# Idle matmuls on a tile that VectorE zeroes, and the last chain of block products in two PSUM banks

## The chip, the cores and the metric

The kernel runs on one core of a Trainium2 chip. The metric is device time in microseconds (us) of one execution; the median of three timed runs is compared. TensorE (PE, with its weight loads shown as PEld), VectorE (DVE), ScalarE (ACT), GpSimd (POOL) and the DMA queue of SyncE (SP) run at the same time and meet at semaphores.

## What is computed

Three stages in float32: causal attention blended with a memory term over 16 heads of 576 positions, a gated pair of dense layers, and a mixture of four experts with ReLU, weighted by normalised domain probabilities.

```
scores = q @ k.T / sqrt(D), causal;  a = softmax(scores);  local = a @ v
attn   = g * (phi(q) @ M_prev) / (phi(q) @ z_prev) + (1 - g) * local
x      = attn as [1152, 512]
x      = ((x @ w1) * (x @ w2)) @ w3 @ w_out
out    = sum over e of p[:, e] * (relu(x @ ew1[e]) @ ew2[e])     # 4 experts, 1024 wide
```

## The kernel before

**Order.** PE, ACT, DVE and POOL follow orders that are written out by hand: the list `FIRST` for the attention and the dense layers, the strings `START`, `CYCLE` and `END` for the experts. In `FIRST`, DMA issues on SP stand in the list too. Each engine executes its instructions in that order and waits where an operand or a buffer is not ready.

**The head.** The zeroing of buffers and the identity matrix `identF` are made by POOL: a memset of `identF`, a larger memset of `mask`, a select that leaves the diagonal. PE opens with 13 transposes of `identF` into a PSUM tile `warm` (lines 206 to 208); nobody reads `warm`. Then come the score products of the first pair of heads, `sc` (line 273), on the operands `qd` and `kd` that SP has loaded: eight float32 products for the first 512 positions, their halves on 64 of the 128 rows each, and two more over the last 64 positions (line 262). A float32 product that is not a transpose stands in the trace as two weight loads and two matmul records. DVE masks each block of scores, takes its minimum (`peaks`, line 289), ACT exponentiates it (line 294), PE transposes the result (`pt`, line 326), ACT copies it out (line 330). SP's load of the query tile two pairs on waits until the first pair's score products have released its buffer; the loads of weights behind it on SP wait with it.

**The experts.** Each expert's two layers are done in halves of its width with both layers cut into 2x2 blocks; a product of 2x2 blocks is made of seven block products. The first 640 tokens are plain in the second layer: five tiles `o` of 128 tokens and 512 columns (`plain_2`, line 1065), with an eviction each that adds to `acc`. The other 512 tokens use seven block products in `block_2` (line 1113). A product named P1 to P7 (F1 to F7 in the last round) is a list of twelve matmuls: two steps `y` (halves of the expert's width), three passes `x` of a float32 product split in high and low parts, and two halves `half` of 128 tokens. Its result stands in an accumulator `o_ps[d]`: d is 0, 1 or 2, each one PSUM bank with the two halves side by side, 256 columns each. The chain d = 0 runs 1, 6, 7, 4: it accumulates through all four, and its bank is added to `acc` after each of them by two evictions, one for each half (`evict`, line 1052, on DVE), scaled by `pr`.

**The banks.** `ps3` has the tags o0 to o4 and R. The plain tiles take o3, o4, o0, o1, o2 for i = 0 to 4; the last round of `block_2` has `banks=(3, 4, 0)`.

**The end.** The string `END` ends with F4: its twelve matmuls, with the halves taken in turn, then the evictions F4x and F4y. In the last round each eviction that completes a block of `acc` is followed by a store, issued by SP (`store`, line 1060). The eviction of the last plain tile (i = 4) is split there: ACT scales it into `part` (line 1086), POOL adds it.

Of the kernel before, what the change touches and what calls it, by code (L numbers as in the profile page):

```python
# [69 lines left out]
def kernel(  # L70
# [16 lines left out]
    nc = tc.nc  # L87
# [80 lines left out]
    A1 = attn.enter_context(tc.tile_pool(name="A1", bufs=1, side="right"))  # L168
    A2 = attn.enter_context(tc.tile_pool(name="A2", bufs=2, side="right"))
    identF = A1.tile([P, P], F32, name="identF")  # L170
    mask = A1.tile([P, S + P], F32, name="mask")
# [34 lines left out]
    warm = turn(psM, [P, 512], F32, "M", 2, "warm")  # L206
    for _ in range(13):
        nc.tensor.transpose(warm[:, 0:P], identF, identF)

# [855 lines left out]
    def plain_2(n):  # L1065

        e, _, j = steps[2 * n]
        q, res = e * NS + j, []
        for i in range(TILES):
            ps = {}  # L1070

            def mm(i, y, x, a, b, first, last, ps=ps):
                def f():
                    if first:
                        ps[0] = ps3.tile([P, 512], F32, tag=f"o{(i + 3) % TILES}", name=f"o{n}_{i}")
                    nc.tensor.matmul(  # L1076
                        ps[0], lhsT=h_of[2 * n + y][x][:, a, i * P : (i + 1) * P], rhs=w2s[q + y][x][:, b, :],
                        start=first, stop=last,
                    )
# [33 lines left out]
    def block_2(n, banks=(0, 1, 2), pre="P"):  # L1113
# [4 lines left out]
        def prod(d, a, b, first):  # L1118
            def mm(y, x, half):
                ia, ib = PASSES[x]  # L1120
                k, h = LOC[b]
                def f():
                    if first and y == x == half == 0:
                        o_ps[d] = ps3.tile([P, 2, HD], F32, tag=f"o{banks[d]}", name=f"ob{n}_{d}")
                    nc.tensor.matmul(  # L1125
                        o_ps[d][:, half], lhsT=h_of[2 * n + y][a][:, ia, half * P : (half + 1) * P],
                        rhs=w2s[q + y][k][:, ib, h * HD : (h + 1) * HD],
                        start=first and y == 0 and x == 0, stop=(y == 1 and x == 2), skip_group_check=True,
                    )
                return f  # L1130
            return [mm(y, x, half) for y in range(2) for x in range(3) for half in range(2)]

        def out_of(d, p, h, first, done=None):
            def half_of(half):
                def f():
                    t = TILES + 2 * p + half
                    evict(acc[t][:, h * HD : (h + 1) * HD], o_ps[d][:, half], t, e, start and first)
                    if last and done:
# [21 lines left out]
    def step(s, seg):  # L1160
# [135 lines left out]
        l41 l42 l43 l44 l45 l4E F50 F51 F52 F60 F61 F62 F53 F54 F55 F5E F63 F64 F65 F6E F20 F21 F22 F23 F24 F25 F2E F70  # L1296
        F71 F72 F73 F74 F75 F7E F30 F31 F32 F33 F34 F35 F3E F40 F41 F42 F43 F44 F45 F4x F4y
    """
# [118 lines left out]
```

## Time and profile before

| | |
|---|---|
| timed runs, median of 3 | 670.37 us (668.66, 670.37, 670.57) |
| the profiled execution, its own time | 668.36 us |
| its span, first to last instruction | 666.6 us |
| PE busy | 658.6 us, 99% of the span |
| DVE, ACT, POOL busy | 500.8, 368.6, 293.2 us |
| chain that ended last, by engine | PE 89%, DVE 6%, ACT 3%, DMA 1%, issue 1% |

The profiled execution's own time is 1.76 us more than its span. The chain that ended last is followed back from the last instruction: at each step the profile goes to the work that released it. An engine's busy time counts from the start of a record to its end; matmul records overlap, so that the distance between starts, and not the length of a record, is the time that each of them takes of the engine.

### The profile page before, as it was taken

To read this page: it belongs to the slowest core of one execution; us is meant where nothing else is said; L and a number is where in the kernel's file an instruction comes from. 1 tells how busy PE (TensorE), PEld (TensorE's weight loads), DVE (VectorE), ACT (ScalarE), POOL (GpSimd) and SP (SyncE) were. 2 spreads that over 40 slices of the span, in tenths; PEclk is the share of its full clock that TensorE was granted. 3 is DMA by queue.
4 is the path that set the end of the run, shared out by engine and by line. 5 is a ranking of instruction groups with operands and counts; after the bars stand their busy time and mean duration, and the time that the engine had idled before them with its cause. 6 is when DMAs were issued, how large, how long until landed. Compare 5 with 4: busy or idle time off the path is not lost.

```text
span 666.6 us, 13313 instructions
## 1 busy us (share of the span) xinstructions
PE 658.6 (99%) x5165; PEld 610.9 (92%) x5165; DVE 500.8 (75%) x1021; ACT 368.6 (55%) x780; POOL 293.2 (44%) x307
## 2 busy tenths in 40 slices
PE   8999999999999999999999999999999999999997
PEld 6778899989999999998899998998998999999997
DVE  5989997898849498577777666776767677676766
ACT  6998987757626364365544454355444444444441
POOL 2037646654443121725353545445454534555410
PEclk9999999999999999999999999999999999999999
DMA  8676266534511040120220211211212102111003
GB/s 280 204 250 191 103 202 180 158 116 159 191 65 64 32 157 3 32 95 1 64 64 2 95 32 31 64 32 33 64 33 64 57 8 94 33 33 32 1 32 111
DMA packets 34767, 57.78 MB, mean 87 GB/s; under 512 B 13456, under 2 KB 14480, under 8 KB 34704
## 3 DMA queue, kind: packets, MB, share of 16 engines
q1 hardware_dynamic: 34704, 56.93, 26.8%
q8 instruction: 40, 0.66, 0.4%
q14 instruction: 23, 0.19, 0.1%
HBM read 50.37 MB, written 6.55 MB: 85 GB/s over the span
## 4 chain that ended last, share of the span: by engine, by line
PE 89%; DVE 6%; ACT 3%; issue 1%; DMA 1%; POOL 0%; SPq 0%; DVEq 0%; POOLq 0%; ACTq 0%
PE o L1076 16%; PE Z L1184 15%; PE ob L1125 12%; PE c L608 8%; PE Q L1184 7%; PE ab L558 7%; PE wacc L494 5%; PE Zb L901 4%; PE R L1184 4%; PE pt L326 2%; PE Qb L901 2%; PE sc L273 2%; PE a L349 1%; DVE P L289 1%; PE Rb L901 1%
## 5 line engine op out<-in xcount | busy, mean ns | idle before, releaser
L1076 PE MATMUL o<-w,h 128*128 128x512 f32 x480 | 122.6, 393 | 0.0
L124 POOL TENSOR_TENSOR w<-r,w 128x512 fp32r<-128x512 f32 x48 | 68.1, 1425 | 97.8 <-ACT w L756 97.8
L1076 PEld LDWEIGHTS o<-w,h 128*128 128x128 f32 x480 | 85.3, 188 | 14.6 <-DVE w L127 0.2
L1125 PE MATMUL ob<-w,hS 128*128 128x256 f32 x384 | 55.2, 282 | 0.0
L558 PE MATMUL ab<-xT,ws 128*128 128x288 f32 x384 | 53.5, 297 | 0.0
L608 PE MATMUL c<-hT,W 128*128 128x288 f32 (+2 forms) x384 | 53.2, 295 | 0.0
L558 PEld LDWEIGHTS ab<-xT,ws 128*128 128x128 f32 x384 | 51.4, 188 | 0.7 <-issue 0.2
L608 PEld LDWEIGHTS c<-hT,W 128*128 128x128 f32 x384 | 51.8, 188 | 0.1
L1125 PEld LDWEIGHTS ob<-w,hS 128*128 128x128 f32 x384 | 51.0, 190 | 0.1
L1184 PE MATMUL Z<-X0T,w 128*128 128x320 f32 x288 | 50.4, 310 | 0.3
L494 PE MATMUL wacc<-wo,w3s 128*128 128x512 f32 x192 | 49.8, 403 | 0.0
L1047 ACT ACTIVATE h<-tt 128x320 fp32r<-128x320 f32 x48 | 22.6, 472 | 47.4 <-DVE tt L1220 21.7
L1056 DVE SCALAR_TENSOR_TENSOR acc<-ob,pr,acc 128x256 f32<-128x256 f32 x104 | 44.1, 476 | 5.9 <-PE ob L1125 5.9
L127 DVE TENSOR_TENSOR w<-r,w 128x512 fp32r<-128x512 f32 x64 | 47.1, 747 | 0.0
L1050 DVE SCALAR_TENSOR_TENSOR h<-tt,h 128x320 fp32r<-128x320 f32 x48 | 27.2, 566 | 25.8 <-ACT h L1047 25.8
L1184 PEld LDWEIGHTS Z<-X1T,w 128*128 128x128 f32 x288 | 40.4, 188 | 4.8 <-DVE X1T L127 0.8
L1125 PE MATMUL ob<-w,hA 128*128 128x256 f32 x288 | 44.3, 282 | 0.0
L1184 PEld LDWEIGHTS Z<-X0T,w 128*128 128x128 f32 x288 | 42.9, 188 | 1.1 <-ACT tt L1205 0.7
L1184 PE MATMUL Z<-X1T,w 128*128 128x256 f32 x288 | 42.1, 282 | 0.4 <-DVE X1T L127 0.4
L1205 ACT COPY tt<-Z 128x320 f32<-128x320 f32 (+1 forms) x32 | 12.8, 400 | 53.4 <-PE Z L1184 53.4
L494 PEld LDWEIGHTS wacc<-wo,w3s 128*128 128x128 f32 x192 | 34.3, 188 | 7.9 <-POOL w3s L124 0.8
L1207 DVE TENSOR_TENSOR tt<-tt,Q 128x320 f32<-128x320 f32 (+1 forms) x32 | 14.5, 453 | 35.2 <-ACT tt L1205 35.1
(198 smaller groups left out, 1585.6 us busy)
## 6 DMA issues: line engine op xcount, KB each, us to landing
w3r<-in_moe_w_tiles_dram SPq DMA_DIRECT2D x16, 512.0 KB, 4.0
wr<-in_moe_w_tiles_dram SPq DMA_DIRECT2D x16, 512.0 KB, 4.0
r<-in_moe_w_tiles_dram SPq DMA_DIRECT2D x32, 256.0 KB, 2.9
r<-in_moe_w_dram SPq DMA_DIRECT2D x32, 256.0 KB, 2.9
wor<-in_moe_w_out_dram SPq DMA_DIRECT2D x8, 512.0 KB, 5.1
wf<-tf SPq DMA_DIRECT2D x16, 256.0 KB, 4.2
wr<-wf SPq DMA_DIRECT2D x16, 256.0 KB, 2.9
qd<-in_q_cols_dram SPq DMA_DIRECT2D x8, 352.0 KB, 4.4
```

Of the source, the lines that this page charges most:

```text
L124: nc.gpsimd.tensor_sub(dst, src, r32(hi))
L127: nc.vector.tensor_sub(dst, src, r32(hi))
L494: nc.tensor.matmul(wacc[u], lhsT=w3s[u][:, a, c, :], rhs=wo[4 * g + c][:, bb, :], start=(c == 0 and x == 0), stop=(c == 3 and x == 2),)
L558: nc.tensor.matmul(ps[:, 0:HS], lhsT=self.ws[u][:, wi, kk, :], rhs=xT[b, kk][:, xi, a * HS : (a + 1) * HS], start=(n == 0), stop=(n == 3 * ...
L608: nc.tensor.matmul(st["ps"], lhsT=Wt[kk][:, wi, d * P : (d + 1) * P], rhs=hT[kk][:, xi, t0 : t0 + tw], start=(kk == 0 and x == 0), stop=(k ...
L901: nc.tensor.matmul(st[d], lhsT=b1_set[m][a][:, wi, kk, :], rhs=BX[b][:, xi, kk, :], start=first and kk == 0 and x == 0, stop=(kk == 1 and ...
L1047: nc.scalar.activation(h, src, AF.Relu)
L1050: nc.vector.scalar_tensor_tensor(out=h[:, 1], in0=src, scalar=0.0, in1=r32(h[:, 0]), op0=ALU.max, op1=ALU.subtract)
L1056: nc.vector.scalar_tensor_tensor(out=dst, in0=src, scalar=pr[:, t, e : e + 1], in1=dst, op0=ALU.mult, op1=ALU.add)
L1076: nc.tensor.matmul(ps[0], lhsT=h_of[2 * n + y][x][:, a, i * P : (i + 1) * P], rhs=w2s[q + y][x][:, b, :], start=first, stop=last,)
L1125: nc.tensor.matmul(o_ps[d][:, half], lhsT=h_of[2 * n + y][a][:, ia, half * P : (half + 1) * P], rhs=w2s[q + y][k][:, ib, h * HD : (h + 1) ...
L1184: nc.tensor.matmul(ps, lhsT=w1s[q][a][:, wi, kk, :], rhs=X[c, b][:, xi, kk, :], start=first and kk == 0 and x == 0, stop=(kk == 1 and x == ...
```

## The change

**The head.** A new tile `zw` of 128x128 float32 is zeroed by DVE, ahead of the other buffers. The 13 transposes of `identF` become 18 products of `zw` with its own first 64 columns.

**The last round's chain d = 0.** Its accumulator becomes two tiles of one bank each: half 0 in o3, half 1 in o2. To clear o2, the last plain tile of the last round (i = 4) takes o4 in place of o2 (`own`). Other rounds keep one bank for both halves.

**The last product.** F4's twelve matmuls are ordered by halves: six for half 0, then six for half 1. F4x, the eviction of half 0, is moved in front of F43 in `END`.

```diff
+    zw = A1.tile([P, P], F32, name="zw")
+    nc.vector.memset(zw, 0.0)
     identF = A1.tile([P, P], F32, name="identF")
...
     warm = turn(psM, [P, 512], F32, "M", 2, "warm")
-    for _ in range(13):
-        nc.tensor.transpose(warm[:, 0:P], identF, identF)
+    for _ in range(18):
+        nc.tensor.matmul(warm[:, 0:SB], lhsT=zw, rhs=zw[:, 0:SB], start=True, stop=True)
...
+        def own(i):
+            return 4 if i == 4 and e == E - 1 and j > 0 else (i + 3) % TILES
+
...
-                        ps[0] = ps3.tile([P, 512], F32, tag=f"o{(i + 3) % TILES}", name=f"o{n}_{i}")
+                        ps[0] = ps3.tile([P, 512], F32, tag=f"o{own(i)}", name=f"o{n}_{i}")
...
                     if first and y == x == half == 0:
-                        o_ps[d] = ps3.tile([P, 2, HD], F32, tag=f"o{banks[d]}", name=f"ob{n}_{d}")
+                        if last and d == 0:
+                            o_ps[d] = [ps3.tile([P, 512], F32, tag=f"o{z}", name=f"ob{n}_{d}_{z}")[:, 0:HD] for z in (3, 2)]
+                        else:
+                            ps = ps3.tile([P, 2, HD], F32, tag=f"o{banks[d]}", name=f"ob{n}_{d}")
+                            o_ps[d] = [ps[:, z] for z in range(2)]
                     nc.tensor.matmul(
-                        o_ps[d][:, half], lhsT=h_of[2 * n + y][a][:, ia, half * P : (half + 1) * P],
+                        o_ps[d][half], lhsT=h_of[2 * n + y][a][:, ia, half * P : (half + 1) * P],
...
+            if last and b == "T4":
+                return [mm(y, x, half) for half in range(2) for y in range(2) for x in range(3)]
             return [mm(y, x, half) for y in range(2) for x in range(3) for half in range(2)]
...
-                    evict(acc[t][:, h * HD : (h + 1) * HD], o_ps[d][:, half], t, e, start and first)
+                    evict(acc[t][:, h * HD : (h + 1) * HD], o_ps[d][half], t, e, start and first)
...
-        F71 F72 F73 F74 F75 F7E F30 F31 F32 F33 F34 F35 F3E F40 F41 F42 F43 F44 F45 F4x F4y
+        F71 F72 F73 F74 F75 F7E F30 F31 F32 F33 F34 F35 F3E F40 F41 F42 F4x F43 F44 F45 F4y
```

On PE at the start of the program, before (a row is one instruction or a run of like ones; behind a name stands its buffer number, in brackets what it waits for):

```order
L208 MATMUL warm_113<-identF_84 128x128 [waits Pool_49]
L208 MATMUL warm_113<-identF_84 128x128 x12
L273 MATMUL sc0_0_161<-kd0_147,qd0_145 128x128 [waits DMAHW1_49,DMAHW0_49]
L273 MATMUL sc0_0_161<-kd0_147,qd0_145 128x128
L273 MATMUL sc0_0_161<-kd0_147,qd0_145 128x256 x2
```

The same place after:

```order
L210 MATMUL warm_115<-zw_84 128x64 [waits DVE_49]
L210 MATMUL warm_115<-zw_84 128x64 x17
L275 MATMUL sc0_0_168<-kd0_154,qd0_152 128x128 [waits DMAHW1_49,DMAHW0_49]
L275 MATMUL sc0_0_168<-kd0_154,qd0_152 128x128
L275 MATMUL sc0_0_168<-kd0_154,qd0_152 128x256 x2
```

The idle matmuls now wait for DVE in place of POOL, there are five more of them, they have 64 columns, and they still stand ahead of the first score products.

On PE at the end of the program, products F3 (accumulator `ob15_2`) and F4 (`ob15_0`), before (`hA30`, `hS30` belong to step y = 0, `hA31`, `hS31` to y = 1):

```order
L1125 MATMUL ob15_2_8073<-w2_14_1_7710,hS30_7821 128x256 x6
L1125 MATMUL ob15_2_8073<-w2_15_1_7742,hS31_7928 128x256 [waits Activation_49]
L1125 MATMUL ob15_2_8073<-w2_15_1_7742,hS31_7928 128x256 x5
L1125 MATMUL ob15_0_7956<-w2_14_3_7862,hA30_7820 128x256 [waits DVE_49]
L1125 MATMUL ob15_0_7956<-w2_14_3_7862,hA30_7820 128x256 x5
L1125 MATMUL ob15_0_7956<-w2_15_3_7974,hA31_7927 128x256 x6
```

The same place after (`ob15_0_3` is half 0 in bank o3, `ob15_0_2` half 1 in o2):

```order
L1135 MATMUL ob15_2_8081<-w2_14_1_7717,hS30_7828 128x256 x6
L1135 MATMUL ob15_2_8081<-w2_15_1_7749,hS31_7935 128x256 x6
L1135 MATMUL ob15_0_3_7963<-w2_14_3_7869,hA30_7827 128x256 [waits DVE_49]
L1135 MATMUL ob15_0_3_7963<-w2_14_3_7869,hA30_7827 128x256 x2
L1135 MATMUL ob15_0_3_7963<-w2_15_3_7982,hA31_7934 128x256 x3
L1135 MATMUL ob15_0_2_7964<-w2_14_3_7869,hA30_7827 128x256 [waits DVE_49]
L1135 MATMUL ob15_0_2_7964<-w2_14_3_7869,hA30_7827 128x256 x2
L1135 MATMUL ob15_0_2_7964<-w2_15_3_7982,hA31_7934 128x256 x3
```

Twelve matmuls stay twelve; half 0 is complete six matmuls earlier, and each half waits for the eviction of its own bank alone.

On DVE at the end of the program, the last four evictions, before:

```order
L1056 SCALAR_TENSOR_TENSOR acc2_4506<-ob15_2_8073,pr_60,acc2_4506 128x256 [waits DVE_49,PE_49]
L1056 SCALAR_TENSOR_TENSOR acc2_4506<-ob15_2_8073,pr_60,acc2_4506 128x256 [waits DVE_49]
L1056 SCALAR_TENSOR_TENSOR acc3_4507<-ob15_0_7956,pr_60,acc3_4507 128x256 [waits PE_49]
L1056 SCALAR_TENSOR_TENSOR acc3_4507<-ob15_0_7956,pr_60,acc3_4507 128x256
L1412 UNCONDITIONAL_BRANCH
```

The same place after:

```order
L1058 SCALAR_TENSOR_TENSOR acc2_4513<-ob15_2_8081,pr_60,acc2_4513 128x256 [waits DVE_49,PE_49]
L1058 SCALAR_TENSOR_TENSOR acc2_4513<-ob15_2_8081,pr_60,acc2_4513 128x256 [waits DVE_49]
L1058 SCALAR_TENSOR_TENSOR acc3_4514<-ob15_0_3_7963,pr_60,acc3_4514 128x256 [waits PE_49]
L1058 SCALAR_TENSOR_TENSOR acc3_4514<-ob15_0_2_7964,pr_60,acc3_4514 128x256 [waits PE_49]
L1424 UNCONDITIONAL_BRANCH
```

The order of the evictions is the same; the last two wait for PE one by one, in place of both for the end of the whole product.

## Rows read from the trace of the kernel before

**Rows 1.** Stretches; busy us of PE, PEld, DVE, ACT, POOL; PEclk; DMA share; GB/s.

```profile
15.00:20.00 5.00, 4.78 (x36) 3.52 (x36) 4.88 (x19) 5.00 (x13) 0.72 (x1) 1.00 0.96 297
30.00:40.00 10.00, 9.78 (x102) 7.15 (x99) 9.82 (x32) 10.00 (x20) 1.89 (x2) 1.00 0.86 259
400.00:500.00 100.00, 100.00 (x673) 94.14 (x672) 70.14 (x135) 46.39 (x105) 51.24 (x56) 1.00 0.14 43
```

**Rows 2.** Chain that ended last, head: start us, us, what.

```profile
1.98 3.03 PE warm L208 x13
...
8.91 1.18 PE sc L262 x4
...
21.50 0.17 DVE gm L586
...
34.60 0.92 PE sc L273 x4
```

**Rows 3.** Timeline of the head: start us, us, engine, line, operation, operands, [idle before].

```profile
0.73 0.20 POOL masks.py:197 MEMSET identF<- 128x128 f32 x1 [0.29 <-POOLq L1377]
...
4.95 3.96 PE L273 MATMUL sc<-kd,qd 64*128 64x128 f32 x16
...
6.76 0.29 DVE L289 CUSTOM_DVE_ANT_0 P<-sc,mask 128x128 f32<-128x128 f32 x1 [0.96 <-PE sc L273]
...
7.09 2.55 ACT L294 ACTIVATE P<-P,mn 128x128 f32<-128x128 f32 x6 [2.58 <-DVE mn L289]
...
11.02 0.78 ACT L294 ACTIVATE P<-P,mn 128x576 f32<-128x576 f32 x1 [0.23 <-DVE mn L289]
```

**Rows 4.** PE records by form, 4.94 to 8.9 us, then 10.87 to 13.3 us.

```profile
L273 PE MATMUL sc<-kd,qd 64*128 64x384 f32 x4 | 1.5, 844 | 0.0
L273 PE MATMUL sc<-kd,qd 64*128 64x512 f32 x4 | 1.2, 698 | 0.0
...
L273 PE MATMUL sc<-kd,qd 64*128 64x512 f32 x4 | 1.1, 632 | 0.0
L273 PE MATMUL sc<-kd,qd 64*128 64x384 f32 x4 | 0.8, 482 | 0.0
```

**Rows 5.** Weight loads by form, 1.9 to 8.8, then 9 to 30 us; one chain piece.

```profile
L273 PEld LDWEIGHTS sc<-kd,qd 64*128 64x128 f32 x16 | 2.3, 326 | 1.1 <-issue 0.9
...
L349 PEld LDWEIGHTS a<-v,pT 128*64 128x64 f32 x135 | 4.1, 137 | 0.2 <-DVE tf_wo L156 0.2
...
L382 PEld LDWEIGHTS b<-mz,phi 128*128 128x128 f32 x8 | 1.0, 190 | 0.0
...
39.91 0.89 PE b L382 x8
```

**Rows 6.** Waits of SP in the first 60 us: total us, times, longest.

```profile
SPq L200 <- PE sc L262: 4.2, 1, 4.2
```

**Rows 7.** The end: timeline of ACT, PEld, DVE and SP.

```profile
656.11 0.68 ACT L1086 ACTIVATE part<-o,pr 128x512 f32<-128x512 f32 x1
...
656.81 1.51 PEld L1125 LDWEIGHTS ob<-w,hA 128*128 128x128 f32 x12
...
661.26 1.60 PE L1125 MATMUL ob<-w,hA 128*128 128x256 f32 x12
...
661.47 0.88 DVE L1056 SCALAR_TENSOR_TENSOR acc<-ob,pr,acc 128x256 f32<-128x256 f32 x2 [0.56 <-PE ob L1125]
662.90 0.88 DVE L1056 SCALAR_TENSOR_TENSOR acc<-ob,pr,acc 128x256 f32<-128x256 f32 x2 [0.56 <-PE ob L1125]
...
663.41 0.81 SPq L1063 DMA_DIRECT2D out_dram<-acc  x2
```

**Rows 8.** The end: chain that ended last; stores' time to landing.

```profile
654.22 8.66 PE ob L1125 x72
...
662.90 0.48 DVE acc L1056
...
DMA to landing us min/median/max: 1.7/2.0/2.4
```

## The prediction

> **What bounds the kernel now.** I read the stretches first. From 400 to 500 us PE is busy for 100.00 of 100 us; in the head it is not the bound: from 15 to 20 us ACT is busy for all 5.00 us and DVE for 4.88, from 30 to 40 us DVE for 9.82 of 10 [rows 1]. The chain that ended last says the same in order: idle matmuls from 1.98 us, the first score products, then ACT and DVE until the chain returns to PE at 34.60 us for good [rows 2]. So a shift of ACT's work in the first 12 us travels through ACT to 21.5 us, through DVE to 34.6, and then through PE to the end. In the head the reader is to see three places: DVE masks the first scores at 6.76 us, ACT has six exponentials from 7.09 to 9.64, and its next one on the chain, at 11.02, came after an idle time of only 0.23 us [rows 3].
>
> The second thing to see in the head is the speed of PE. The column PEclk reads 1.00, which is the level of 2.4 GHz, but the records speak against it: records of score products of 384 columns take 844 ns in the first set and 482 in the second; those of 512 columns, which come last in a set, take 698 and 632 [rows 4]. So PE runs at the level of 1.2 GHz through the idle transposes and the first products, and rises while the products of 512 columns run, near 8.2 us: some 6.2 us after the first idle transpose and 3.2 us after the first product (4.95 [rows 3]).
>
> **The change part by part: the head.** The memset of a 128x128 tile on POOL takes 0.20 us from 0.73 [rows 3]; DVE's masking of a 128x128 block takes 0.29, so zw is there at 0.93 to 1.02 and PE can begin at about 1.0 in place of 1.98 [rows 2]. The memset is first in DVE's queue; the next instruction there waits for an exponential of a loaded operand, so it costs DVE nothing. The first real transposes now carry the wait for POOL's identity, which PE had at 1.98 [rows 2]: nothing.
>
> What do 18 idle products take? Each float32 product is two records, as the sixteen records of the eight first score products show [rows 3], so there are 36 weight loads of 128 columns, each followed by a matmul of 64 columns. A load of 64 columns takes 137 ns and one of 128 columns 190 [rows 5]; the difference, 53 ns for 64 columns, makes 106 ns for 128 at the high level. The matmul beside it is shorter: eight records of 130 columns take 0.89 us, 111 ns each [rows 5], so 64 columns take some 54. The load is the longer of the two and sets the pace. At the low level loads of 128 columns take 326 against 190 ns [rows 5]; twice 106 is 213 ns, which I take. No row has loads as the bound at the low level: the pace lies between 106 ns (the matmuls, at half speed) and 320 (load and matmul one after the other). I take 213 because it is the one that follows from the rows of loads.
>
> When does the level rise? If the idle products count as the score products do, 3.2 us after 1.0: at 4.2. If it is the time since PE's first work of any kind, 6.2 us after: at 7.2. At 4.2 us 15 of 36 records are done and 21 remain at 107 ns: the idle products end at 6.45. At 7.2 us 29 are done: they end at 7.94. Score products can then start, 1.5 to 3.0 us later than before, but at the high level. From the first product to the first exponential it was 2.14 us (4.95 to 7.09 [rows 3]); the products of 128 and 256 columns, 384 of the 1280 columns that took 3.96 us, are 1.2 us of that, 1.4 since all of them ran at the low level, and half of this is saved: 2.14 - 0.7 = 1.4. From the first exponential to the end of ACT's work before 11.02 nothing changes (3.7 us). So the head moves by 6.45 + 1.4 - 7.09 - 0.23 = +0.5 us at the one end and 7.94 + 1.4 - 7.09 - 0.23 = +2.0 at the other; the 0.23 is ACT's idle time, which absorbs as much. I take +1.4, near the middle. SP's load of a later query tile waits 4.2 us for the first pair's products [rows 6], and the weights and keys behind it wait with it; with the first sixteen records in some 2.2 us at the high level and the last four in 1.18 [rows 2], these products end 9.8 to 11.3 against 10.09, which is less of a shift than ACT's, so SP adds nothing.
>
> The Trainium skill, in "TensorE: Matmul & The Clock Gate", Part 4 (PE-mode transpose), says that a transpose does not count as TensorE's activity for the clock as a product does. The trace agrees so far: PE was busy with transposes for 3 us and the level did not rise during them. By that rule alone the earlier end, +0.5 us, would hold.
>
> **The change part by part: the end.** Of the last twelve matmuls, from 661.26 and 0.12 us apart (72 in 8.66 us), half 0 is complete after six, at about 662.15. DVE is then busy with F3's evictions (661.47, two in 0.88 us) until 662.35, so F4x runs to 662.83 and is over before the last matmul ends at 662.88 [rows 7, 8]. F4y then starts at 662.90, where F4x started before; the two took 0.88 us in a row and one takes 0.48 [rows 7, 8], so the last eviction ends 0.40 us earlier. SP's last two stores were issued back to back from 663.41 in 0.81 us [rows 7], each behind its eviction; now F4x's goes out near 662.9 and the last one at 663.41, so that the last landing, 1.7 to 2.4 us behind its issue [rows 8], moves by 0.40 too. I take -0.4; the bounds are 0 (if the last store lands no earlier) and -0.5 (if the two stores also stop delaying each other).
>
> Three new waits go with it. F2, the chain d = 1, uses o4, which now holds the last plain tile, so it waits for ACT's `part`, which ends at 656.79; the loads of F2 began at 656.81 [rows 7]. With the time of a semaphore the delay is 0.05 us at most; behind it on PE stands everything to the end. F7 now waits for each half's eviction by itself, which can only be earlier. The last plain tile in o4 waits for the eviction of plain tile 1, long done. I take 0 for all, with +0.1 as their bound.
>
> **Sum.** 668.36 + 1.4 - 0.4 = 669.4 us, with 668.4 to 670.0 from the ends above; 670.3 if a wait at the end adds its bound and the last store nothing. The sum stands against the profiled execution (668.36), which is 2.0 us below the median of the timed runs (670.37). Two of these runs lie 2 us above the profiled one; a rise that comes later in some executions would do that, and would do it less after the change, but no row shows it. Against the median the forecast is -0.15%.
>
> **Rivals.** First, **the idle products are too thin to raise the level**: in each record PE streams for 107 of 213 ns, while in the score products and the transposes matmul follows on matmul. For it: nothing in the trace rises under such a stream. Against it: weights move all the time. Then all 36 records run at the low level, 36 x 0.213 = 7.7 us, to 8.7; the first exponential comes 2.14 us later, at 10.8; the head moves by 10.8 - 7.09 - 0.23 = +3.5 us, and by up to 2 us more if the rise falls behind the next four records (1.18 us at the high level [rows 2], as much again at half speed) and the transposes that follow. It gives 671.5 to 673.5, about 672.5: slower. It decides from the point at which the first score product starts after 8.5 us.
>
> Second, **the loads do not set the pace**: a record then takes 107 ns even at the low level, 36 take 3.85 us, and the idle products end at 4.85, before the score products began. With the level up at 4.2 the first exponential comes at 4.85 + 1.4 = 6.25, a gain of 0.84; with 7.2 the gain is 0.1. It gives 667.1 to 667.9, about 667.4: faster. Against it stands the difference of 53 ns between loads of 64 and 128 columns [rows 5]. The Trainium skill, in "TensorE: Matmul & The Clock Gate", LDWEIGHTS (loading the stationary operand), gives a load as its columns over 1.2 GHz, 107 ns for 128 at either level, and by that rule this rival would hold.
>
> Third, **the head does not reach the end**: DVE or PE has enough slack before 34.6 us to absorb the shift, and the change does only what its end part says, 668.36 - 0.4 = 668.0. Against it: ACT and DVE stand at 5.00 of 5 and 9.82 of 10 us [rows 1].
>
> **How the numbers follow.** Forecast 0.52, thin products 0.24, no load bound 0.14, head without effect 0.10. A measurement of this kernel can tell some 0.3% from no change, 2.0 us: faster is below 668.36, slower above 672.38. The forecast's own range, 668.4 to 670.3, lies within that, but for 0.04 below; the third rival sits just under the bound and gives half of its chance to faster, as does all of the second: faster 0.04 + 0.14 + 0.05 = 0.23, rounded to 0.22. Thin products give a little over half of their chance to slower, 0.13, and 0.01 comes from the other cases: 0.14. Same is the rest, 0.64. The predicted time is the forecast's, 669.4. The range reaches from 667.2 to 672.2: it leaves out about 0.04 of the second rival below and 0.13 of the first above.
>
> **What would show it.** In the profile of the changed kernel: PE's first record near 1.0 us; 36 idle records, and their end, at 6.4 to 7.9 (forecast), 8.7 (thin) or 4.9 (no load bound); the mean of the first products of 384 columns near 482 ns (forecast) or near 844 (thin); the first six exponentials from about 8.5 us in place of 7.09; ACT's next one at about 12.4 in place of 11.02; the chain's return to PE 1.4 us after 34.60. At the end: F4's two evictions 0.6 us apart, and the last store issued some 0.5 us after the last matmul, in place of 0.9. The forecast is wrong if the idle products end before 6 or after 8.5 us, or if the shift at 11 us is not found again at 35 us.

## The result and the profile after the change

The changed kernel takes 675.29 us (median of 6 runs, 674.24 to 676.26), the kernel before 669.93 beside it (6 runs): a ratio of 1.0083 (95% interval 1.0070 to 1.0095), slower by 5.4 us. The forecast was 669.4 and its range ended at 672.2, so it was wrong, and the time lies above the 671.5 to 673.5 of the first rival too. The profiled execution has 676.26 us and a span of 674.5.

PE in the head of the changed kernel (timeline; start us, us, engine, line, operation, operands, records, [idle before]):

```profile
1.05 7.94 PE L210 MATMUL warm<-zw 128*128 128x64 f32 x36 [1.05 <-DVE zw L171]
8.92 4.64 PE L275 MATMUL sc<-kd,qd 64*128 64x128 f32 x16
13.49 1.39 PE L264 MATMUL sc<-kd,qd 128*128 128x288 f32 x4
```

The tile of zeros is ready as early as forecast (first record at 1.05, not 1.98 [rows 2]). The 36 records then take until 8.99, and the first score product starts at 8.92 in place of 4.95 [rows 3]. The records by form from 8.9 to 13.5 us (busy us, mean ns) tell at which level PE ran:

```profile
L275 PE MATMUL sc<-kd,qd 64*128 64x512 f32 x4 | 1.9, 1057 | 0.0
L275 PE MATMUL sc<-kd,qd 64*128 64x384 f32 x4 | 1.5, 844 | 0.0
```

Before, those of 384 columns took 844 ns and those of 512 columns 698 in the first set, the last of them at the higher level already [rows 4]. Now both forms are at the level of 1.2 GHz. The trace's record of the granted clock gives the rise at 13.84 us, after all sixteen records; it was 8.10 before. So the new idle products not only took longer: the level did not rise during them, nor in the sixteen records after them.

ACT behind it (same columns), and SP's wait for the first pair's products (total us, times, longest):

```profile
11.07 2.55 ACT L296 ACTIVATE P<-P,mn 128x128 f32<-128x128 f32 x6 [6.81 <-DVE mn L291]
15.83 0.78 ACT L296 ACTIVATE P<-P,mn 128x576 f32<-128x576 f32 x1 [1.09 <-DVE mn L291]
```

```profile
SPq L202 <- PE sc L264: 9.3, 1, 9.3
```

The first exponential is 3.98 us later (11.07 against 7.09), the one of 576 columns 4.81 later (15.83 against 11.02 [rows 3]), SP waits 9.3 us instead of 4.2 [rows 6]. In the chain that ended last (start us, us, what) `gm` stood at 21.50 [rows 2] and is now 4.79 us later:

```profile
1.05 7.94 PE warm L210 x36
8.99 4.57 PE sc L275 x16
13.56 1.34 PE sc L264 x4
...
26.29 0.18 DVE gm L588
```

The chain runs through the idle products now, where it ran through the transposes: whatever they last too long, the kernel waits for.

Every later instruction of ACT can be set against the same one of before: the lag is 5.11 us at 33 us of the program before, 5.55 at 166, 6.12 at 189, 8.04 at 255, and 7.90 at the end. Most of the step to 8.04 is one wait near 249 us (same columns as SP's; 0.8 us before):

```profile
ACT w L758 <- DMA r<-in_moe_w_tiles_dram: 2.7, 1, 2.7
```

The end part did its work on DVE, as this timeline shows:

```profile
669.37 1.27 DVE L1058 SCALAR_TENSOR_TENSOR acc<-ob,pr,acc 128x256 f32<-128x256 f32 x3 [0.68 <-PE ob L1135]
670.80 0.48 DVE L1058 SCALAR_TENSOR_TENSOR acc<-ob,pr,acc 128x256 f32<-128x256 f32 x1 [0.17 <-PE ob L1135]
```

F4x now runs behind F3's evictions, in the group of three, and only one eviction is left after the last product. From ACT's `part` to the end of the last eviction it is 7.27 us (664.01 to 671.28), against 7.67 before (656.11 to 663.78 [rows 7]): 0.40 less. But the stores gave it back. From the end of the last eviction to the end of the span it is 3.2 us (674.5 - 671.28) and was 2.8 (666.6 - 663.78). This is SP's issue of the stores (duration ns min/median/max, first and last start us), and their time to landing:

```profile
L1065 SPq DMA_DIRECT2D out_dram<-acc x12: 333/390/1513, 658.6 to 671.8; - x12
...
DMA to landing us min/median/max: 1.8/2.2/4.1
```

Before, the longest landing was 2.4 [rows 8] and no issue behind 655 us took over 0.4 us. The landing of 4.1 us is not what the end waited for: that store was issued at 667.0 us and had landed by 671.1, and the last four took 1.8 to 2.0. What reached the end is the issue of 1.51 us: it held SP from 668.75 to 670.27, the four stores behind it went out 0.48 to 0.49 us apart, and the last one at 671.81, 0.53 us after the end of its eviction (0.06 before). What stood beside these stores is the last experiment's subject.

### The profile page after: what moved, and what is told of

It reads as the page before. It is cut to its first block, busy times and chain, and to the rows that moved or that the text cites. A ratio compares the mean times of both kernels' runs of the same rounds, so it can differ in the third digit from the quotient of the medians.

```text
span 674.5 us, 13362 instructions
## 1 busy us (share of the span) xinstructions
PE 664.9 (99%) x5188; PEld 616.3 (91%) x5188; DVE 503.7 (75%) x1022; ACT 368.7 (55%) x780; POOL 291.9 (43%) x307
## 4 chain that ended last, share of the span: by engine, by line
PE 87%; ACT 6%; DVE 3%; DMA 2%; issue 1%; SPq 0%; DVEq 0%; ACTq 0%
PE o L1082 16%; PE Z L1196 15%; PE ob L1135 12%; PE c L610 7%; PE Q L1196 7%; PE ab L560 6%; PE wacc L496 5%; PE R L1196 4%; PE Zb L903 3%; PE pt L328 2%; PE a L351 2%; PE sc L275 2%; PE Qb L903 1%; ACT P L296 1%; ACT pT L332 1%; PE warm L210 1%
## 5 line engine op out<-in xcount | busy, mean ns | idle before, releaser
L296 ACT ACTIVATE P<-P,mn 128x128 f32<-128x128 f32 (+4 forms) x72 | 37.5, 584 | 7.9 <-DVE mn L291 7.9
```

Of the source, the lines that this page charges most:

```text
L296: nc.scalar.activation(Pt[i, x], Pt[i, x], AF.Exp, bias=one, scale=-1.0)
```

## The experiments

The table gives for each the idle work in front (records of products are written weight columns x moving columns), from the profiled execution the start of the first score product, the rise of the level by the trace's clock record, the start of ACT's 576-column exponential, and ACT's lag against the kernel before at 33, 189 and 291 us (an instruction's start minus that of the same one before), and the ratio of the times with its interval.

| kernel | idle work | score | rise | 576 | lag 33/189/291 | ratio |
|---|---|---|---|---|---|---|
| before | 13 transposes | 4.95 | 8.10 | 11.02 | 0 | 1 |
| after | 36 of 128x64 | 8.92 | 13.84 | 15.83 | 5.1/6.1/8.0 | 1.0083 [1.0070, 1.0095] |
| e8, after again | the same | 8.92 | 14.10 | 15.96 | 5.0/7.5/7.3 | one run, 675.2 us |
| e2, without end part | the same | 8.92 | 11.85 | 14.88 | 4.4/6.8/8.2 | 1.0088 [1.0063, 1.0113] |
| e4 | 18 of 128x64 | 5.08 | 9.93 | 11.96 | 0.9/1.7/2.0 | 1.0005 [0.9988, 1.0021] |
| e12 | 80 of 128x64 | 18.30 | 21.12 | 24.22 | 13.2/14.4/15.3 | one run, 683.0 us |
| e3 | 18 of 128x128 | 5.18 | 7.05 | 10.86 | -0.2/1.6/2.1 | 0.9978 [0.9963, 0.9993] |
| e11, e3 again | the same | 5.19 | 5.58 | 10.33 | -0.2/0.6/0.4 | 0.9993 [0.9980, 1.0007] |
| e5 | 38 of 128x128 | 7.71 | 5.74 | 12.67 | 1.8/3.6/4.1 | 1.0046 [1.0030, 1.0063] |
| e6 | 36 of 64x64 | 5.08 | 5.05 | 10.03 | -0.4/1.2/2.1 | 1.0016 [1.0000, 1.0032] |
| e10, e6 again | the same | 5.08 | 6.50 | 10.73 | 0.0/1.1/1.5 | 1.0029 [1.0016, 1.0041] |
| e13 | 18 of 64x64 | 4.61 | 10.09 | 11.79 | 0.8/3.0/3.4 | 0.9997 [0.9982, 1.0011] |
| e14 | 26 of 64x64 | 4.71 | 4.03 | 9.67 | -1.4/0.1/1.3 | 1.0006 [0.9988, 1.0024] |
| e7 | none | 4.83 | 8.85 | 11.34 | 0.4/2.4/2.3 | 1.0015 [1.0001, 1.0028] |
| e1, end part alone | 13 transposes | 4.94 | 6.26 | 10.54 | -0.5/1.3/1.9 | 0.9979 [0.9964, 0.9994] |
| e9, e1 again | the same | 4.94 | 6.93 | 10.64 | -0.4/0.6/0.9 | 0.9999 [0.9988, 1.0011] |

The lags are measured against one execution of the kernel before, which took 668.36 us where the median of six is 669.93. So a lag of 1 to 2 us at 291 us need not be a loss: e1 and e3, whose ratios are under 1, show 1.9 and 2.1.

### The two halves apart

The first keeps the transposes and changes the end only; the second changes the idle products and leaves the end as it was.

```diff
e1, e9  -    for _ in range(18):
e1, e9  -        nc.tensor.matmul(warm[:, 0:SB], lhsT=zw, rhs=zw[:, 0:SB], start=True, stop=True)
e1, e9  +    for _ in range(13):
e1, e9  +        nc.tensor.transpose(warm[:, 0:P], identF, identF)
...
e2      -            if last and b == "T4":
e2      -                return [mm(y, x, half) for half in range(2) for y in range(2) for x in range(3)]
```

(e1 and e9 also drop `zw` and its memset; e2 also takes back the banks and the order of the last chain.)

> The kernel before with the end part of the change alone (13 transposes of identF as before, zw left out). Theory (the loss is all in the head, the end gains what the prediction worked out): 0.4 us less than before, ratio 0.9994, the last two evictions apart and the last store issued some 0.4 us earlier behind the last matmul. Rival (the two banks or the new wait of F2 cost something at the end): no gain or up to 0.5 us more, with an idle time of PE before F2 or F7.

> The kernel before with the head part of the change alone (zw, 18 products of 64 columns). Theory: the whole loss and 0.4 us more than the changed kernel, some 5.8 us over before, ratio 1.0086; 36 idle records at 213 ns each, the first score product near 8.9 us. Rival (part of the loss is at the end): clearly less than 5.4 us over before.

The whole loss is the head's: with the head part alone the ratio is 1.0088, with the end part alone 0.9979. The end part's DVE rows (timeline) are as forecast in e1, and here the stores from 662 us on land as they did before (under the two rows; the last line is SP's issue of the stores):

```profile
663.22 1.27 DVE L1056 SCALAR_TENSOR_TENSOR acc<-ob,pr,acc 128x256 f32<-128x256 f32 x3 [0.64 <-PE ob L1133]
664.66 0.48 DVE L1056 SCALAR_TENSOR_TENSOR acc<-ob,pr,acc 128x256 f32<-128x256 f32 x1 [0.17 <-PE ob L1133]
```

```profile
DMA to landing us min/median/max: 1.7/1.8/2.2
...
L1063 SPq DMA_DIRECT2D out_dram<-acc x10: 332/348/401, 654.9 to 665.2; - x10
```

From `part` (657.87) to the last eviction's end it is 7.27 us again, and the last store was issued 0.03 us after it. A second comparison of the same kernel (e9) gave 0.9999 [0.9988, 1.0011], so 0.4 us fits both intervals and neither measures it.

### Which idle products raise the level

Four kernels with the end part change the idle products alone:

```diff
e3, e11  -    for _ in range(18):
e3, e11  -        nc.tensor.matmul(warm[:, 0:SB], lhsT=zw, rhs=zw[:, 0:SB], start=True, stop=True)
e3, e11  +    for _ in range(9):
e3, e11  +        nc.tensor.matmul(warm[:, 0:P], lhsT=zw, rhs=zw, start=True, stop=True)
e4       -    for _ in range(18):
e4       +    for _ in range(9):
e6, e10  -        nc.tensor.matmul(warm[:, 0:SB], lhsT=zw, rhs=zw[:, 0:SB], start=True, stop=True)
e6, e10  +        nc.tensor.matmul(warm[0:SB, 0:SB], lhsT=zw[:, 0:SB], rhs=zw[:, 0:SB], start=True, stop=True)
e12      -    for _ in range(18):
e12      +    for _ in range(40):
```

> The changed kernel with 9 idle products of 128 columns in place of 18 of 64: 18 records, as many columns in all, done near 4.9 us. Theory (the idle products of the change were too thin to raise the clock level, and too many): matmul follows on matmul, the level rises during or shortly behind the idle products, the first score records of 384 columns take near 482 ns in place of 844, the first exponential comes before 7.1 us, and the time is 1 to 2 us below before. Rival (idle products do not bring the rise forward, whatever their form; it comes some time behind the first score products): score records of 384 columns at 844 ns and the time of before less 0.4 us.

> The changed kernel with 9 idle products of 64 columns in place of 18: half the records, done near 4.9 us, so that the score products start when they did before. Theory (delay of the score products is the larger part of the loss; thin products do not raise the level): the level as before, the time of before less 0.4 us, within 1 us. Rival (the thin products themselves harm, or what replaces the transposes is missed for the level): still 2 us or more over before, with the level rising later than in before.

e3 and e4 have the same number of loads, the same pace of 213 ns and, within 0.1 us, the same start of the score products. Only the moving side differs, and with it the score records, first of e4 and then of e3 (records by form in their score products):

```profile
L275 PE MATMUL sc<-kd,qd 64*128 64x512 f32 x4 | 1.9, 1057 | 0.0
L275 PE MATMUL sc<-kd,qd 64*128 64x384 f32 x4 | 1.5, 844 | 0.0
```

```profile
L275 PE MATMUL sc<-kd,qd 64*128 64x384 f32 x4 | 1.0, 589 | 0.0
L275 PE MATMUL sc<-kd,qd 64*128 64x512 f32 x4 | 1.0, 589 | 0.0
```

With 64 moving columns all of them run at 1.2 GHz; with 128 the level is up in the middle of the set. The exponential of 576 columns is 1.1 us later in e4 (11.96 against 10.86; 1.6 against the 10.33 of e11). That is what the missing rise costs ACT by itself, without a delay.

> The change with 64 instead of 128 columns in each idle product's weight load (the moving side keeps its 64 columns, 36 records), end part as in the change. If the load of 128 columns sets the pace of 213 ns, a load of half as many columns gives about 107 ns, and the 36 records end near 4.9 us, before the raw tiles are there: score products from about 5.1 us, first exponential near 7.3 us, and a time of 668 to 670, the loss of the change gone but for the level. If the pace is that of the instruction whatever its columns, the records end near 8.7 us and the time stays at 675. For the level: if it waits for moving columns, the rise comes as late as with nine thin products (9.9 us; 576-column exponential near 12); if it waits for the matrix unit to be in work without gaps, it comes near 6 to 7 us (576-column exponential near 10.7).

e6 keeps the 64 moving columns and halves the load. Its 36 records take 4.1 us in place of 7.94:

```profile
1.04 4.10 PE L210 MATMUL warm<-zw 128*64 128x64 f32 x36 [1.04 <-DVE zw L171]
5.08 2.43 PE L275 MATMUL sc<-kd,qd 64*128 64x128 f32 x16
```

The records start 107 ns apart where those of the changed kernel start 213 apart: the load of 128 columns had set the pace. And the level rises at 5.05, under products of the same 64 moving columns. So 64 moving columns as such do not keep the level down; the two streams differ in the load alone, and by it in the pace.

> The change with 40 instead of 18 idle products (80 records). In all looks at thin idle products so far (18 or 9 of them) the level rose 2.9 to 5.2 us after the first score product and never before it, but the streams ended at 4.7 or 8.6 us and it rose between 9.9 and 14.1 us, so a stream that only needs longer isn't excluded. Theory 'products of 64 columns behind loads of 128 never bring the rise forward': all 80 records 213 ns apart at the lower level, the last start at 1.05 + 79 x 0.213 = 17.9 us, score products from 18.3 us, the rise at 21.2 to 23.5 us, first exponential near 20.4, and a time near 675.2 + 9.4 = 684 to 685. Rival 'they do, only later': the level rises inside the stream, between 10 and 14 us, the records after it come closer together, all score products run at the higher level, and the score products start at 14 to 16.5 us, a time near 680 to 682.

```profile
1.04 17.33 PE L210 MATMUL warm<-zw 128*128 128x64 f32 x80 [1.04 <-DVE zw L171]
18.30 3.80 PE L275 MATMUL sc<-kd,qd 64*128 64x128 f32 x16
```

But for the first gap of 265 ns, all 80 records are 213 to 214 ns apart, the last at 17.95 us, and the level rises at 21.12, 2.8 us after the first score product. So this stream does not raise the level late: in 17 us it did not raise it. The time, 683.0, is a little under the 684 to 685 expected.

### Delay without the missing rise, and no idle work at all

```diff
e5   -    for _ in range(18):
e5   -        nc.tensor.matmul(warm[:, 0:SB], lhsT=zw, rhs=zw[:, 0:SB], start=True, stop=True)
e5   +    for _ in range(19):
e5   +        nc.tensor.matmul(warm[:, 0:P], lhsT=zw, rhs=zw, start=True, stop=True)
e7   -    zw = A1.tile([P, P], F32, name="zw")
e7   -    nc.vector.memset(zw, 0.0)
e7   -    for _ in range(18):
e7   -        nc.tensor.matmul(warm[:, 0:SB], lhsT=zw, rhs=zw[:, 0:SB], start=True, stop=True)
```

> 19 idle products with a moving side of 128 columns on the zeroed tile (38 records), end part as in the change: about the delay of the changed kernel, but from the stream after which the level rose early (nine of them: rise at 7.05 us). Theory 'the loss is the number of 128-column weight loads at the lower level, plus what the score products lose at it': the level rises inside the idle stream, near 7 us; 28 records at 213 ns to there and 10 at half of that put the last start near 8.1 us, the score products near 8.4, all of them at the higher level, the first exponential near 10.4, the 576-column one near 13.5, and the time near 671 to 672. Rival 'only the start of the score products counts, the level in them is nothing': the same 3.2 us later than with nine, so first exponential and 576-column one both 3.2 us after 7.33 and 10.86. Rival 'the level rises only some us after score products have begun, whatever stood ahead': 38 times 213 ns put the start at 9.2 us, first exponential at 11.4, the time at 675 to 676.

```profile
1.04 6.73 PE L210 MATMUL warm<-zw 128*128 128x128 f32 x38 [1.04 <-DVE zw L171]
7.71 2.43 PE L275 MATMUL sc<-kd,qd 64*128 64x128 f32 x16
...
12.67 0.77 ACT L296 ACTIVATE P<-P,mn 128x576 f32<-128x576 f32 x1
```

Here the level rises inside the idle stream, at 5.74, earlier than the 7 us I expected; the records go from 213 to 112 ns, and the products start at 7.71, not 8.4. The exponential of 576 columns is 1.65 us later than before (expected some 2.5), yet the time of 672.07 is the one expected: more was lost further on (lag 1.8 at 33 us, 4.1 at 291).

> No idle products and no zeroed tile, end part as in the change. The raw tiles set the start of the score products then, as they do with 13 transposes (4.94 us): start from 4.2 to 4.95 us. Theory 'idle products are worth only what they bring the rise forward': the rise comes 2.9 to 4.9 us after the first score product, as it did behind thin products, at 7.5 to 9.9 us; 576-column exponential near 11.5 to 12, and a time as with nine thin products, 669 to 670.5. Rival 'thin idle products help too': slower than nine thin ones by over 1 us, 671 and more. Rival 'the level is nothing': as with nine dense ones, 668.2.

```profile
4.83 1.65 PE L271 MATMUL sc<-kd,qd 64*128 64x128 f32 x8 [4.83 <-DMA kd<-in_k_cols_dram]
```

Without idle work the raw tiles set the start, 4.83 us, the level rises 4.0 us later, and the kernel takes 670.1, as expected. This row also says how much idle work has any use: what ends before 4.8 us is free, every record after it is a delay. The changed kernel's stream ended 4.2 us after that.

### What else grew behind the head

> The changed kernel once more, unaltered, for a second look at two things that its profile showed once: the rise of the level 4.9 us after the first score product, and the 2 us that it lost near 249 us behind a transfer of weights that took 6.0 us to land. If the rise is as late by the kernel itself, it comes at 13 to 14 us again; if it varies by execution, between 11 and 14. If the late landing belongs to the change, the wait of ScalarE there is over 2 us again and the lag at the end near 8 us; if not, it is under 1 us and the lag at the end 5.5 to 6.5 us, as in the kernel with the head part alone.

The rise came at 14.10, as late as in the other execution. The wait near 249 us did not come again:

```profile
ACT w L758 <- DMA r<-in_moe_w_tiles_dram: 0.4, 1, 0.4
```

But the wait does not belong to one execution: e2, which has the same head, shows it as well, with one part of the transfer 1.1 us behind the others as in the changed kernel:

```profile
ACT w L758 <- DMA r<-in_moe_w_tiles_dram: 2.1, 1, 2.1
```

In e8 the lag at 291 us was 7.3 all the same, not 5.5 to 6.5 (nor was it that in e2: 8.2). This execution had lost 1.9 us between 33 and 96 us (lag 4.95 to 6.85) and 0.8 between 166 and 189.

A second thing was odd. e6 has an earlier head than e1, but its time was 1.7 us above e1's. Further comparisons of e1, e6 and e3 were to tell whether that was spread:

> The end part alone again, with more runs and beside the two kernels whose idle products also end before the raw tiles arrive. All three have a head that is within 0.6 us of that of the kernel before (576-column exponential at 10.5, 10.9 and 10.0 us), yet the one with narrow weight loads gave 670.2 and the other two 668.2 to 668.4. Theory 'below about half a microsecond the head is lost in the waits for transfers between 60 and 255 us, and the difference was spread': all three within 1 us of each other, 668 to 669.5, this one 0.4 us under the kernel before (the end part). Rival 'what the idle products are has an effect further on': the narrow ones again 1.5 to 2 us above this one.

> 36 records with weight loads of 64 columns, again. By the first theory 668 to 669.5 and within 1 us of the end part alone; by the rival 670 to 670.5. In its profile the level should rise within half a microsecond of the end of the idle products again (5.05 us the first time), whatever the time is.

> Nine products of 128 columns (18 records), again. By the first theory 668 to 669.5. By the rival, too, 668.2 (it was the fastest). If it stays under the kernel before with its whole interval, by some 0.5 to 0.9 us, a zeroed tile and dense idle products are a version that beats both kernels, though by no more than the end part alone gives.

It was not: 668.24, 670.06 and 667.84 us beside 668.33 of the kernel before. The first theory fell. In e6 and e10 alike the lag grows by 1.1 to 1.2 us between 166 and 189 us of the program before, where e1, e3, e9 and e11 lose nothing. ACT waits there for a tile of weights, in e9 and then in e10 (timeline, and under it the time of that transfer from issue to landing):

```profile
178.70 0.68 ACT L149 ACTIVATE tu<-wr 128x512 uint32<-128x512 uint16 x1 [0.17 <-DMA wr<-in_moe_w_tiles_dram]
```

```profile
DMA to landing us min/median/max: 4.3/4.3/4.3
```

```profile
179.41 0.66 ACT L149 ACTIVATE tu<-wr 128x512 uint32<-128x512 uint16 x1 [1.54 <-DMA wr<-in_moe_w_tiles_dram]
```

```profile
DMA to landing us min/median/max: 5.7/5.7/5.7
```

The trace has a landing event for each of a transfer's sixteen parts. In e10 fifteen had landed by 178.1 us, and the last landed at 179.3, 1.2 us behind. From 177.1 to 178.2 us one packet of 16 KB of queue q8, which brings instructions, was under way; in e9 the fetch of that place came at 178.9. The page counts 40 packets of q8 for kernels with 5152 to 5178 PE records and 41 for those with 5188 and more, the changed kernel among them. This is its line (packets, MB, share of 16 engines), and then e9's:

```profile
q8 instruction: 41, 0.67, 0.4%
```

```profile
q8 instruction: 40, 0.66, 0.4%
```

The same shows over the whole program, as a tendency. From 60 us on, in all sixteen traces, a packet of 16 KB of q8 was under way beside 535 transfers (between their issue and the landing of their fifteenth part); in 178 of them the last part came over 0.5 us behind the fifteenth. Of the 1812 other transfers 58 had such a part. Near 249 us, too, the packet ran from 253.2 us in the changed kernel and in e2, and from 254.5 in e8, where no part was late.

In all kernels with 41, but for e12, the last one falls among the last stores: the changed kernel's runs from 668.4 to 669.9 us, and one part of each of the three stores issued from 667.0 to 668.3 us lands 1.7 us behind the others (1.1 to 1.8 in two to four stores of e2, e5, e6, e8 and e10). SP's issue of the store behind them took 1.2 to 1.5 us in the changed kernel, e5, e6 and e10; in e8 the last stores themselves landed late. From the last eviction's end to the span's end it is 2.9 to 3.3 us in these five and 2.64 to 2.67 in the other kernels with the end part. e2, without the end part, lost nothing there (2.78; before 2.79). These are the lines of q8 (packets, MB, share of 16 engines) and of the stores (count, KB each, median us to landing) from 660.5 us on, of the changed kernel, and then that of the stores of e1, which has no line of q8 there:

```profile
q8 instruction: 1, 0.02, 0.6%
...
out_dram<-acc SPq DMA_DIRECT2D x8, 128.0 KB, 2.7
```

```profile
out_dram<-acc SPq DMA_DIRECT2D x8, 128.0 KB, 1.8
```

To see whether the number of idle instructions or the narrow form costs the time, e6's products are cut to 9 and to 13:

```diff
e13  -    for _ in range(18):
e13  +    for _ in range(9):
e14  -    for _ in range(18):
e14  +    for _ in range(13):
```

> Nine products with weight loads and moving sides of 64 columns (18 records). With 36 such records the time was 670.1 twice, 1.8 us above the kernels whose heads are as early. What the profiles show there: one more fetch of 16 KB of instructions over the program (41 against 40 with 18 records or fewer), one of them at 177 us beside a weight transfer that then took 5.7 us in place of 4.3, and one at 662 us beside the last stores. Theory 'the number of idle instructions moves the fetches, and two of them then meet transfers that somebody waits for': with 18 records 40 fetches again, none between 661 us and the end, the weight transfer of that place at 4.3 to 4.5 us, last stores 1.7 to 1.8 us to landing, and a time of 667.8 to 668.8. Rival 'the narrow form itself costs 1.8 us': 669.6 to 670.2. The idle records end near 3.1 us here and the score products start with the raw tiles, 4.8 to 5.0 us; should the level rise late (576-column exponential after 11.2 us, as without idle products), up to 1 us more by either.

> The same with 13 products (26 records), between the two counts. By the theory of the fetches the time follows their number, not the number of products: 667.8 to 668.8 if the profile has 40 and none beside the last stores, 669.4 to 670.2 if it has 41. By the rival of the form about 669, half of the 1.8 us.

e13 clears the form as such: its ratio is 0.9997 [0.9982, 1.0011], where 1.8 us more would be 1.0027. e14's 1.0006 [0.9988, 1.0024] does not tell the two theories apart. Both have 40 fetches, none beside the last stores, the stores at 1.8 us to landing and the weight transfer at 4.4. The times expected of the fetches, 667.8 to 668.8, did not come out (669.44 and 669.64); but the kernel before took 669.10 beside them, not the 668.33 beside e9 to e11, and the ratios are what 667.8 to 668.8 would be over 668.33 (0.9992 to 1.0007). PE in e13 and then in e14:

```profile
1.04 2.18 PE L210 MATMUL warm<-zw 128*64 128x64 f32 x18 [1.04 <-DVE zw L171]
4.61 4.64 PE L275 MATMUL sc<-kd,qd 64*128 64x128 f32 x16 [1.38 <-DMA kd<-in_k_cols_dram]
```

```profile
1.04 3.03 PE L210 MATMUL warm<-zw 128*64 128x64 f32 x26 [1.04 <-DVE zw L171]
4.71 2.43 PE L275 MATMUL sc<-kd,qd 64*128 64x128 f32 x16 [0.63 <-DMA kd<-in_k_cols_dram]
```

e13's records were over at 3.2 us, PE then waited 1.38 us for the tiles, and the sixteen score records took 4.64 us: the level rose late, at 10.09, which was allowed for. In e14 it rose at 4.03, before the products, and they took 2.43. e14 had the earliest head of all, 1.35 us ahead of the kernel before at the 576-column exponential, and its lag goes from -1.4 at 33 us to +1.3 at 291: the lead was used up in waits for weights. A fetch from 176.4 to 177.5 us has a part in that: the transfer that e10 waited for landed in 4.4 us, but of the two behind it (`wf`) one part each came 0.6 us late, and ACT's next instruction waited for one of them:

```profile
178.97 0.67 ACT L150 ACTIVATE tf<-wr 128x512 f32<-128x512 f32 x1 [0.56 <-DMA wf<-tf]
```

The changed kernel has the same wait, of 0.59 us, behind a fetch at the same place of its program. So a packet of code beside a transfer often goes with a late part here, but I didn't isolate it: no kernel has as many idle records as e6 and 40 fetches. Where the rest of the 1 to 2 us goes between 60 and 255 us stays open.

## Why the prediction was wrong, point by point

**The tile of zeros, the count and the pace were right.** First record at 1.05 (forecast 1.0), 36 records, 213 ns apart at the lower level. The second rival, that the loads don't set the pace, falls with that, and e6 shows it from the other side: half the columns, half the pace. The rule that the prediction cited for it, from the Trainium skill, "TensorE: Matmul & The Clock Gate", LDWEIGHTS (loading the stationary operand), is 107 ns for 128 columns. The page names no level; the prediction took it for both. These rows disagree at the lower level (213); after the rise in e5 the records, 112 ns apart, are near it.

**The step that failed is "When does the level rise?"** It took a rise at 4.2 to 7.2 us, "if the idle products count as the score products do", or by the time since PE's first work. Neither alternative contained the third: that they don't count. The first rival named that, and the trace of before held no row against it. The forecast's halving of 21 or 7 of the 36 records and of the first score products hung on this one step, and all of it fell away: the products started at 8.9 us in place of 6.5 to 7.9, and the level rose at 13.84 in place of 4.2 to 7.2.

**The first rival's mechanism was right, its price too low.** It had the end of the stream at 8.7 (8.99 by the row), the first exponential at 10.8 (11.07), the head at +3.5 with up to 2 more (+4.8 at the 576-column exponential and 5.1 at 33 us, against ACT's 0.23 us of slack), and 672.5 as the time, 2.8 us under the median measured. The largest part of that is the base, which the forecast shares: every sum starts from the profiled execution, 668.36, and this is 1.6 us under the median of six runs, 669.93 (the prediction says that it stands 2.0 under its three). From the median the rival's range would be 673.0 to 675.0 and the forecast 670.9, so the forecast fails by either base. The part that was called "up to 2 us more" was 1.3, 1.4 and 0.4 us (the 576-column exponential at 15.83, 15.96 and 14.88 against 11.02, less 3.5). The shift came to the end nearly one for one, as the sum had it: 5.1 us at 33 us, 5.4 between the medians. (ACT's lag of 7.9 us at the end is these 5.4, the 1.6 of the base, and 1.0 by which the profiled execution of the changed kernel, 676.26, lies over its median.) Of the 5.4 us about 5 are the head's, the end gave back 0.4 or nothing, and a remainder under 1 can't be told from the spread of the later waits.

**A slip in the sum.** With the head's upper end, 0.1 for a wait and nothing gained at the end it gives 670.5, not 670.3; nothing hangs on it.

**SP adds nothing** is not contradicted: SP waited 9.3 us in place of 4.2, 5.1 more, which is the shift that ACT has anyway.

**The end part.** The evictions moved by 0.40 us, as forecast, and the three waits cost what the bounds said: the last plain tile in o4 puts the loads behind it at 664.75, 0.06 us after `part`'s end (0.02 before [rows 7]), and the last 72 products take 8.66 us in both. The stores followed in e1, and not in the changed kernel: there an issue of 1.51 us held up the last four, and the 0.4 us were gone. No row of before shows SP held like that, so the bound of 0 was the right one to keep.

**The transposes.** The prediction weighed a rule of the Trainium skill (same page, Part 4, PE-mode transpose) that transposes don't count as activity for the clock as products do. The runs speak against it: behind 13 transposes the level rose 1.3 and 2.0 us after the first score product (e1, e9) and 3.2 in before; without idle work it was 4.0 (e7), and 5.5 in e13, whose idle work was long over. Of the three profiled executions of this head, the one in before has the latest rise, and its 3.2 lies among the 2.8 to 5.2 of the thin products, so that row alone could not show it.

**The third rival**, that the head doesn't reach the end, fell for a delay: 5.1 us at 33 us came back as 5.4 between the medians. For a lead it holds rather well: e14's 1.4 us never arrived.

## What to carry to other kernels

Whether idle products raise TensorE's level is a question to the trace, not to the fact that PE is busy: weights of 128 columns with 64 moving ones did not in five profiled executions; 128x128, transposes and 26 or more records of 64x64 brought the rise forward; 18 records of 64x64, over 1.4 us before the first operands, did not. The mean duration of the first real products tells. Size the stream to end when the first operands land, about 4.8 us here, because every record after that delays all that follows. A lead of the head was worth nothing (e14), while lags of 1.8, 5.1 and 13.2 us at 33 us came back as 3.0, 5.4 and 13.9 in the time (e5, the changed kernel, and e12 in one run). No version here is measurably better than the kernel before: nine products of 128 columns with the end part gave 0.9978, with an interval below 1, and 0.9993, with one that holds 1.

## What the runs showed of the hardware

- The level rose 2.8 to 5.2 us after the first score product behind idle products of 128x64, and 4.0 after it with no idle work. Behind 128x128, 64x64 and transposes it rose 3.0 to 6.1 us after the first idle record, except for e13, whose stream was over at 3.2 us (5.5 us after its first score product). The same kernel differs from execution to execution: 5.05 and 6.50 (e6, e10), 7.05 and 5.58 (e3, e11), 6.26 and 6.93 (e1, e9).
- A float32 product's weight load at the lower level paces records at 213 ns for 128 columns and 107 for 64.
- Kernels with 5188 or more PE records fetched 41 packets of 16 KB of code, those with 5178 or fewer 40, and the fetches stand at other places of the program. One such fetch took 0.9 to 2.3 us. One part in sixteen landed over 0.5 us behind the others in 178 of 535 transfers beside such a fetch, and in 58 of 1812 others.
- Behind stores with a part 1.4 to 1.7 us late SP's issue of the next store took 1.2 to 1.5 us in four executions, 0.3 to 0.4 us there in the kernels with 40 packets; in e8, with parts as late, it did not.
